# First-half gate weights in units of 256 columns in a GLA + multiplicative-FFN kernel

## Chip, cores, metric

The kernel runs on one core of a Trainium2 chip. The metric is device time in microseconds. Three runs of the kernel before gave 472.68, 473.71 and 473.98 us; the median is 473.71 us. One further execution was profiled: 475.23 us in all, with a span of 473.5 us from its first to its last instruction.

The engines are called PE (TensorE; its weight loads are listed apart as PEld), DVE (VectorE), ACT (ScalarE), POOL (GpSimd) and SP (SyncE, which here only issues transfers). [...]

## The reference

Two blocks follow each other. The first is a gated linear attention, step by step over a sequence of 768, for 4 batches of 8 heads of 48 channels:

```python
for t in range(S):
    state = alpha[:, :, t, :, None] * state + np.einsum('bhd,bhe->bhde', k[:, :, t], v[:, :, t])
    y[:, :, t] = np.einsum('bhd,bhde->bhe', q[:, :, t], state)
```

Its output, as 3072 tokens of 384 channels (x), goes through a feed-forward block without an activation:

```python
a = x @ w1              # 384 -> 1024
b = x @ w2              # 384 -> 1024
h = a * b @ w3          # 1024 -> 1024
return (h @ w_out).astype(np.float32)
```

q, k, v and alpha are float32. The weights w1, w2, w3 and w_out are float64.

## The kernel before, in words

**Part 1: 25 steps over 24 chunks.** The sequence of each batch is cut into chunks of 128 positions: 6 per batch, 24 in all, n = 0 to 23. The main loop (`for n in range(N + 1)`, L634) handles in step n several chunks at once: the scores of chunk n (`scores`, PE L399, masked on DVE at L402 into a tile `ms`), the transposed q and k of chunk n + 1 (`transposed`, PE L359, copied by ACT at L361), the output of chunk n - 1 (`attend_state`, L419, and `attend`, L425, copied by ACT at L429 into a tile `x`), the state update of chunk n (`outer`, PE L371, DVE L379 or L381), the product of q and k with the decays for chunk n + 2 (`decayed`, DVE L337, which is the first reader of the loaded k and q), and the decays of chunk n + 3 (`decays`, PE L318, L321 or L324, and the exponentials on ACT, L327 and L328). The logarithms of alpha (`logs`, ACT L302 or L294) are taken one step ahead of the decays. For every second chunk POOL carries a scaled state over (`advance`, L388 to L390), with factors that go through DRAM and back (L330, L332, L309, then L345).

**Loads.** SP issues nearly all transfers in one order: at the top of step n the stores of an earlier output (`store`, L283), alpha of chunk n + 5 (`load_a`, L142), k and q of chunk n + 3 (`load_kq`, L148 and L149), and weights. v of chunk n + 2 is loaded by POOL for chunks 3 to 7 (L154), otherwise by SP. Three buffers hold k and q, three the alpha of single chunks (chunks 2 to 7 come in pairs and have their own place), five v (`AHEAD` + 1), two the output tile `x`. Each transfer of SP also waits, by a rotation of eight semaphores, for the landing of the one issued eight before it. A row of q, k, v or alpha is 48 floats, 192 B, in DRAM.

**Weights.** w1 and w2 arrive as float64 and are turned into float32 from their two 32-bit words, and then into three parts: h, a rounded top; l, the remainder; m, a second remainder. One unit is a tile of 128 rows and 512 columns (512 KB; a row is 4096 B): rows `kk` of one matrix, one half of the columns. Its generator (`load_gates`, with `to_fp32`) has five stages: issue the load (L213); take the words apart (DVE L222, L225; ACT L221, L226); combine them (DVE L228, L229, L231); h on ACT (L238); l on DVE (L240), which for the second half of the columns also makes m on DVE (L243). For the first half m is made by PE instead (`third`: two matmuls, L254 and L255, and an ACT copy, L256). `fetch` starts loads so that at most `raws` units are begun; `convert(k)` runs k stages. There are 12 units; the first six are the columns 0 to 511, the others columns 512 to 1023.

**Gates.** The tokens form 8 groups g of 384 (three chunks). Once a group's x is complete in DRAM it is loaded (`load_x`, L441) and split in three by `split_x` into the tile `x3`: ACT L447, DVE L448, DVE L449. A gate tile f is 128 of the 1024 columns for one group: for w1 and for w2 nine matmuls (`products`, L455), ACT L464 and DVE L466 take the result out of PSUM, DVE L503 multiplies the two and the product is stored. In part 1 the gate tiles f = 0 to 3 (first half) of the groups 0 to 3 are threaded into the steps in pieces of nine matmuls by `run`. Group 0 starts in step 7 (`FIRST` is 6): two pieces after the transposes, then three more; three in step 8. All eight pieces need units of the first half, and every one of them needs x3 in all three parts.

**Part 2** holds the other gate tiles, the folding of w3 with w_out, and the output products. The change doesn't touch it.

**Order.** The program order is that of the loop, with `after_marks` adding some orders by hand; the Tile framework then fixes the queue of every engine when the program is built. So which instruction stands before which on an engine is known without a run.

Of the kernel before, what the change touches and what calls it, by code (L numbers as in the profile page):

```python
# [48 lines left out]
def kernel(  # L49
# [26 lines left out]
    CW = 512  # L76
    AHEAD = 4
    LATE = 10
# [54 lines left out]
    def load_a(n):  # L133
        if paired(n):
            if n % 2 == 0:
                b, c = divmod(n, NCH)
                x = pairs[n // 2 % 2]
                nc.sync.dma_start(out=x.rearrange("p h s d -> p h (s d)"), in_=alpha[b, :, ds(c * C, 2 * C), :].rearrange("h (p s) d -> p h (s d)", s=2))
                st["a", n] = st["a", n + 1] = x
        elif n < N:  # L140
            st["a", n] = inp.tile([C, H, D], FP32, tag="ac", name="ac")
            nc.sync.dma_start(out=st["a", n], in_=rows(alpha, n))  # L142
# [92 lines left out]
    def load_gates(i, kk, half):  # L235
        w = yield from to_fp32(None, (moe_w1, moe_w2)[i][ds(kk * C, C), ds(half * CW, CW)])
        h, l, m = (w12[half][:, x, i, kk, :] for x in range(3))
        nc.scalar.activation(h, w, AF.Copy, scale=(1.0 - 2.0 ** -13) / P)  # L238
        yield
        mark["l"] = nc.vector.scalar_tensor_tensor(l, h.bitcast(FP32), -P, w, op0=ALU.mult, op1=ALU.add).ins  # L240
        done.append((i, kk, half))
        if half:
            nc.vector.scalar_tensor_tensor(m, h.bitcast(FP32), P + 1.0, w, op0=ALU.mult, op1=ALU.subtract)  # L243
        else:
            thirds.append((m, h, l))

    weights, begun, thirds, done = deque(), deque(), deque(), []

    def third(count):

        for _ in range(count):
            m, h, l = thirds.popleft()
            p = bank()
            nc.tensor.matmul(p, signs[:, 0], h, start=True, stop=False)  # L254
# [109 lines left out]
    def outer(n):  # L364
# [9 lines left out]
        if n % 2:  # L374
            to = st["T", n] = work.tile([C, NP, D], FP32, tag="tmp", name="tmp")
        else:
            to = Ts[1][:, :, 0:D]
# [44 lines left out]
    def attend(n):  # L422
        (y, heads), ms, vc = st.pop(("y", n)), st.pop(("ms", n)), st.pop(("v", n))
        for j, i, to in heads:
            nc.tensor.matmul(to, vc[:, 2 * j + i, :], ms[:, i, j, :], start=(n % NCH == 0 and j % HP == 0),  # L425
                             stop=(j % HP == HP - 1), skip_group_check=True)
        x = work.tile([C, HP, 2, C], FP32, tag="x", name="x")
        for i in range(2):
# [180 lines left out]
    FH = CW // C  # L609
    for half in range(DF // CW):  # L610
        for kk in range(KM):
# [22 lines left out]
    for n in range(N + 1):  # L634
# [3 lines left out]
        if n != 1:  # L638
            load_a(n + 5)
        raws = (3, 3, 3, 3, 2, 2, 3, 3)[n] if n < 8 else 4  # L640
        for m in (n + 3,) * (n <= FIRST) + (n + 4,) * (n >= FIRST):
            load_kq(m)
            if n < FIRST - 2:
                fetch(raws)
            if n >= FIRST:
                load_v(m - 1)
        if n:
# [19 lines left out]
        if n == FIRST:  # L667
            with after_marks("l", ("qkT", n + 1)):
                split_x(0, 0)
            fill.extend(gate(0, f) for f in begin[n - 3][1])  # L670
        pieces = ((3, 3, 2, 0) if n > FIRST + 3 else (0, 3, 3, 0))[(n - FIRST) % 4] if n >= FIRST else 0
        if n == 0:
# [6 lines left out]
        marks = (*[("qkT", n + 1)] * (n < N - 1), *[("qk", n + 1), ("ms", n)] * early, *["x3"] * (n - 2 in begin and n > FIRST))  # L679
        if n < N - 2 and n != FIRST:  # L680
            with after_marks(*marks):
                convert(2 if n == 0 else 1, raws)
        advance(n)
# [3 lines left out]
        third(ready)  # L687
        run(pieces > 0)
        if early:
            with after_marks(*marks):  # L690
                convert(1, raws)
# [5 lines left out]
        if n == 4:  # L697
            load_x(0)
        convert(early and n > 0, raws)
        run(pieces > 1)  # L700
# [5 lines left out]
        if n == FIRST:  # L706
            with after_marks("x3", ("e", n + 3)):
                convert(2, raws)
        elif n < N - 2:
            convert(early or n % 3 == 0, raws)  # L710
        if n == FIRST - 1:
            assert len(done) == 2 * KM
        run(pieces > 2)
# [96 lines left out]
```

## Time and profile before

| | |
|---|---|
| three runs, median | 473.71 us (472.68 to 473.98) |
| profiled execution | 475.23 us, span 473.5 us |
| PE busy / weight loads busy | 457.5 us (97%) / 432.1 us (91%) |
| DVE / ACT / POOL busy | 358.3 / 278.7 / 78.7 us |
| first matmul of a gate (L455) | 59.93 us |
| DVE L449, first x3 complete | 60.42 us, 1.35 us long |
| moved by DMA | 80.29 MB, mean 170 GB/s |
| transfers of w1, w2 and w3 | 28 of 512 KB, median 5.4 us from issue to landing |
| loads of k, of q | 24 each of 192 KB, median 5.1 and 5.6 us |

Busy time of an engine is the time its instructions take; a wait counts as idle, and the profile names what ended it. Matmuls are pipelined, so that their busy time can overlap: 1152 instances of L455 with 338 ns each stand in the trace about every 0.18 us. The chain of waits follows the work that ended last backwards from the end of the program.

### The profile page before, as it was taken

What the parts mean: (1) busy time and instruction counts of PE and PEld (TensorE: products, weight loads), DVE (VectorE), ACT (ScalarE), POOL (GpSimd) and SP (SyncE); (2) the same over time, 40 slices, a digit from 0 to 9 for tenths busy, and PEclk for the clock granted to TensorE, in tenths of its full rate; (3) what the DMA queues carried; (4) which work ended last, traced back from release to release, by engine and by line L of the source; (5) the groups of instructions that cost most, each with busy time, mean ns of one, the idle gap of its engine ahead of it and who ended that gap; (6) DMA issues with size and microseconds to landing.
All of it is one profiled execution on the core that took longest, in us unless ns stands there. A gap on an engine that the chain in (4) does not pass through costs nothing.

```text
span 473.5 us, 10040 instructions
## 1 busy us (share of the span) xinstructions
PE 457.5 (97%) x3848; PEld 432.1 (91%) x3848; DVE 358.3 (76%) x578; ACT 278.7 (59%) x552; POOL 78.7 (17%) x150
## 2 busy tenths in 40 slices
PE   4997899999999999999999999999999999999996
PEld 2675589899989998999999999999999999999996
DVE  2887797999869787999989968854642877666761
ACT  4676864867768464898877765654453533333330
POOL 5243121113201310222221202111011000000000
PEclk9999999999999999999999999999999999999999
DMA  9999999999999933567675532212013986555511
GB/s 181 245 206 227 227 229 201 250 205 208 202 223 184 280 100 122 152 187 242 205 257 178 189 124 89 96 49 85 33 51 98 256 242 184 166 164 169 173 51 50
DMA packets 145663, 80.29 MB, mean 170 GB/s; under 512 B 96240, under 2 KB 137456, under 8 KB 145616
## 3 DMA queue, kind: packets, MB, share of 16 engines
q1 hardware_dynamic: 139840, 64.44, 54.9%
q0 software_dynamic: 5776, 15.22, 10.2%
q8 instruction: 30, 0.49, 0.5%
q14 instruction: 17, 0.14, 0.1%
HBM read 57.58 MB, written 22.06 MB: 168 GB/s over the span
## 4 chain that ended last, share of the span: by engine, by line
PE 87%; DMA 5%; DVE 2%; issue 2%; SPq 2%; ACT 1%; POOL 1%; POOLq 0%; DVEq 0%; ACTq 0%
PE bank L455 71%; PE bank L425 4%; PE bank L399 4%; PE bank L419 2%; PE bank L359 2%; DMA kq<-in_q_dram 2%; PE bank L557 1%; PE bank L371 1%; PE bank L324 1%; DMA dec<-ends 1%; DMA ends<-e 1%; DMA xd<-x 1%; PE bank L321 1%; SPq L149 1%; DMA ac<-in_alpha_dram 1%
## 5 line engine op out<-in xcount | busy, mean ns | idle before, releaser
L455 PE MATMUL bank<-x,w 128*128 128x384 f32 x1152 | 212.1, 338 | 0.6 <-DVE x L449 0.6
L455 PEld LDWEIGHTS bank<-x,w 128*128 128x128 f32 x1152 | 200.1, 188 | 2.9 <-issue 1.4
L455 PE MATMUL bank<-w3o,ab 128*128 128x384 f32 x576 | 100.2, 336 | 0.0
L455 PEld LDWEIGHTS bank<-w3o,ab 128*128 128x128 f32 x576 | 99.9, 188 | 0.0
L480 ACT ACTIVATE bank<-bank 128x384 f32<-128x384 f32 x96 | 45.8, 477 | 41.3 <-PE bank L455 41.1
L464 ACT ACTIVATE t<-bank 128x384 f32<-128x384 f32 x64 | 31.4, 493 | 56.4 <-PE bank L455 55.4
L530 POOL DMA_DIRECT2D abd<-ab x45 | 26.1, 579 | 144.9 <-DVE ab L516 126.1
L516 DVE TENSOR_TENSOR ab<-bank,r 128x384 f32<-128x384 f32 x44 | 24.4, 554 | 25.4 <-ACT bank L480 15.4
L361 ACT COPY qkT<-bank 128x512 f32<-128x512 f32 x48 | 26.0, 593 | 23.4 <-PE bank L359 23.4
L586 DVE TENSOR_TENSOR ab<-abl,ab 128x1024 fp32r<-128x1024 f32 x24 | 29.4, 1224 | 13.1 <-ACT ab L585 13.1
L585 ACT ACTIVATE ab<-abl 128x1024 fp32r<-128x1024 f32 x24 | 25.5, 1061 | 21.2 <-PE bank L455 18.3
L455 PE MATMUL bank<-wo,w3T 128*128 128x384 f32 x192 | 35.9, 334 | 0.0
L455 PEld LDWEIGHTS bank<-wo,w3T 128*128 128x128 f32 x192 | 33.5, 188 | 0.0
L226 ACT ACTIVATE power<-power,rebias 128x512 uint32<-128x512 uint32 (+1 forms) x36 | 25.1, 699 | 12.4 <-DVE power L225 12.2
L337 DVE TENSOR_TENSOR qk<-kq,e 128x768 f32<-128x768 f32 x24 | 22.9, 953 | 12.4 <-ACT e L328 8.4
L399 PEld LDWEIGHTS bank<-qkT 48*128 48x128 f32 x384 | 24.4, 193 | 8.1 <-issue 2.7
L399 PE MATMUL bank<-qkT 48*128 48x128 f32 x384 | 29.3, 291 | 2.4 <-DVE tmp L381 1.8
L402 DVE TENSOR_TENSOR ms<-bank,keep 128x512 int32<-128x512 int32 x48 | 31.2, 683 | 0.4 <-PE bank L399 0.3
L466 DVE SCALAR_TENSOR_TENSOR o<-bank,t 128x384 f32<-128x384 f32 x24 | 13.4, 557 | 22.1 <-issue 13.7
L587 DVE SCALAR_TENSOR_TENSOR ab<-ab,abl 128x1024 fp32r<-128x1024 f32 x24 | 29.2, 1218 | 0.0
L466 DVE SCALAR_TENSOR_TENSOR r<-bank,t 128x384 f32<-128x384 f32 x40 | 22.0, 553 | 8.8 <-PE bank L455 4.1
L425 PE MATMUL bank<-ms,v 128*64 128x128 f32 x384 | 26.3, 279 | 0.0
(88 smaller groups left out, 582.8 us busy)
## 6 DMA issues: line engine op xcount, KB each, us to landing
raw<-in_moe_w_dram SPq DMA_DIRECT2D x28, 512.0 KB, 5.4
abl<-abd SPq DMA_DIRECT2D x24, 512.0 KB, 4.2
abd<-ab POOLq DMA_DIRECT2D x45, 192.0 KB, 3.0
xT<-xd POOLq DMA_DIRECT2D x9, 576.0 KB, 4.6
kq<-in_k_dram SPq DMA_DIRECT2D x24, 192.0 KB, 5.1
kq<-in_q_dram SPq DMA_DIRECT2D x24, 192.0 KB, 5.6
xd<-x SPq DMA_DIRECT2D x48, 96.0 KB, 4.0
out_dram<-o SPq DMA_DIRECT2D x24, 192.0 KB, 3.3
```

The lines of the kernel that those rows point to most:

```text
L361: mark["qkT", n] = nc.scalar.copy(qkT[:, :, :, ds(DP * half, DP)], tp[half]).ins
L399: nc.tensor.matmul(sc[i][:, j, :], qkT[r, 0, j, :], qkT[r, 1, j, :], start=True, stop=True)
L402: masked = nc.vector.tensor_tensor(ms[:, i].bitcast(I32), sc[i].bitcast(I32), keep_bc, op=ALU.bitwise_and)
L425: nc.tensor.matmul(to, vc[:, 2 * j + i, :], ms[:, i, j, :], start=(n % NCH == 0 and j % HP == 0), stop=(j % HP == HP - 1), skip_group_chec ...
L455: nc.tensor.matmul(p, w[part][i], x[part][i], start=start and part == parts[0] and i == 0, stop=stop and part == parts[-1] and i == n - 1, ...
L464: nc.scalar.activation(t, p1, AF.Copy, scale=(1.0 + 1.0 / P) * scale)
L466: nc.vector.scalar_tensor_tensor(to, p2, scale, t, op0=ALU.mult, op1=ALU.add)
L480: nc.scalar.activation(p, p, AF.Copy, scale=1.0 + 1.0 / P)
L530: (nc.gpsimd if late else nc.sync).dma_start(out=abd[g][:, f, :], in_=ab)
L585: nc.scalar.activation(t[:, 0], ab, AF.Copy, scale=1.0 - 2.0 ** -13)
L586: nc.vector.tensor_sub(t[:, 1], ab, t[:, 0].bitcast(FP32))
L587: nc.vector.scalar_tensor_tensor(t[:, 2], t[:, 0].bitcast(FP32), -1.0 - 1.0 / P, ab, op0=ALU.mult, op1=ALU.add)
```

## The change

The first half of the columns is no longer loaded in six units of 128 rows and 512 columns, but in three units of the columns 0 to 255 and three of the columns 256 to 511 (`load_first`). A unit holds two tiles of 128 rows and 256 columns: rows 0 to 255 of w1; rows 0 to 255 of w2; rows 256 to 383 of both. It takes two transfers of 256 KB with rows of 2048 B, where a unit took one of 512 KB with rows of 4096 B. A unit still has 512 numbers per partition, so the stages of its conversion have the same sizes as before. The first three units suffice for the gate tiles 0 and 1, all six for 2 and 3. The units of the second half are as they were.

The schedule is moved with it. Four `convert` calls in each of the steps 0 to 5 become 2, 2, 3, 3, 2 and 4; the step 6 has 3 instead of 2, step 7 has 5 instead of 1. So 16 stages (four units) are through by step 5 instead of 24 (six units), and the other two units are converted in steps 6 and 7; their `third` is in step 8. Step 7 runs four pieces of gates instead of five, step 8 four instead of three. In the last steps of part 1 (`while begun`) five stages of the second half are left instead of two.

The buffers change too: four for v (`AHEAD` 3), and v of chunk n + 2 instead of n + 3 is loaded in the steps from 6 on; two for the single alpha tiles, one for the tile `tmp` of the state update, four for the output tile `x`.

```diff
@@ -74,7 +74,7 @@
     NG = N // G
     TG = G * C
     CW = 512
-    AHEAD = 4
+    AHEAD = 3
     LATE = 10
     PAIRED = 8
     assert D <= DP and DM % C == 0 and DF % CW == 0 and S % C == 0 and N % G == 0
@@ -138,7 +138,7 @@
                 nc.sync.dma_start(out=x.rearrange("p h s d -> p h (s d)"), in_=alpha[b, :, ds(c * C, 2 * C), :].rearrange("h (p s) d -> p h (s d)", s=2))
                 st["a", n] = st["a", n + 1] = x
         elif n < N:
-            st["a", n] = inp.tile([C, H, D], FP32, tag="ac", name="ac")
+            st["a", n] = inp.tile([C, H, D], FP32, tag="ac", name="ac", bufs=2)
             nc.sync.dma_start(out=st["a", n], in_=rows(alpha, n))
 
     def load_kq(n):
@@ -237,20 +237,28 @@
         h, l, m = (w12[half][:, x, i, kk, :] for x in range(3))
         nc.scalar.activation(h, w, AF.Copy, scale=(1.0 - 2.0 ** -13) / P)
         yield
+        nc.vector.scalar_tensor_tensor(l, h.bitcast(FP32), -P, w, op0=ALU.mult, op1=ALU.add)
+        nc.vector.scalar_tensor_tensor(m, h.bitcast(FP32), P + 1.0, w, op0=ALU.mult, op1=ALU.subtract)
+
+    def load_first(c0, k):
+        part = ds(c0, CW // 2)
+        srcs = [((moe_w1, moe_w2)[i], kk) for i in range(2) for kk in range(KM)][k::KM] if k == KM - 1 else \
+            [((moe_w1, moe_w2)[k], kk) for kk in range(KM - 1)]
+        w = yield from to_fp32(None, *(m[ds(kk * C, C), part] for m, kk in srcs))
+        w = w.rearrange("p (a b) -> p a b", a=2)
+        h, l, m = (w12[0][:, x, :, KM - 1, part] if k == KM - 1 else w12[0][:, x, k, 0:KM - 1, part] for x in range(3))
+        nc.scalar.activation(h, w, AF.Copy, scale=(1.0 - 2.0 ** -13) / P)
+        yield
         mark["l"] = nc.vector.scalar_tensor_tensor(l, h.bitcast(FP32), -P, w, op0=ALU.mult, op1=ALU.add).ins
-        done.append((i, kk, half))
-        if half:
-            nc.vector.scalar_tensor_tensor(m, h.bitcast(FP32), P + 1.0, w, op0=ALU.mult, op1=ALU.subtract)
-        else:
-            thirds.append((m, h, l))
-
-    weights, begun, thirds, done = deque(), deque(), deque(), []
+        thirds.append((m, h, l))
+
+    weights, begun, thirds = deque(), deque(), deque()
 
     def third(count):
 
         for _ in range(count):
             m, h, l = thirds.popleft()
-            p = bank()
+            p = bank().rearrange("p (a b) -> p a b", a=2)
             nc.tensor.matmul(p, signs[:, 0], h, start=True, stop=False)
             nc.tensor.matmul(p, signs[:, 1], l, start=False, stop=True)
             nc.scalar.copy(m, p)
@@ -372,7 +380,7 @@
                                  start=True, stop=True)
 
         if n % 2:
-            to = st["T", n] = work.tile([C, NP, D], FP32, tag="tmp", name="tmp")
+            to = st["T", n] = work.tile([C, NP, D], FP32, tag="tmp", name="tmp", bufs=1)
         else:
             to = Ts[1][:, :, 0:D]
         if n % NCH == 0:
@@ -424,7 +432,7 @@
         for j, i, to in heads:
             nc.tensor.matmul(to, vc[:, 2 * j + i, :], ms[:, i, j, :], start=(n % NCH == 0 and j % HP == 0),
                              stop=(j % HP == HP - 1), skip_group_check=True)
-        x = work.tile([C, HP, 2, C], FP32, tag="x", name="x")
+        x = work.tile([C, HP, 2, C], FP32, tag="x", name="x", bufs=4)
         for i in range(2):
             copied = nc.scalar.copy(x[:, :, i], y[i])
         ends_of_part1[1] = copied.ins
@@ -607,7 +615,9 @@
                 fill.popleft()
 
     FH = CW // C
-    for half in range(DF // CW):
+    assert KM == 3 and CW % 4 == 0
+    weights.extend(load_first(c0, k) for c0 in (0, CW // 2) for k in range(KM))
+    for half in range(1, DF // CW):
         for kk in range(KM):
             weights.extend(load_gates(i, kk, half) for i in range(2))
 
@@ -637,13 +647,13 @@
             load_x(loads[n])
         if n != 1:
             load_a(n + 5)
-        raws = (3, 3, 3, 3, 2, 2, 3, 3)[n] if n < 8 else 4
+        raws = (2, 3, 2, 3, 3, 3, 3, 3)[n] if n < 8 else 4
         for m in (n + 3,) * (n <= FIRST) + (n + 4,) * (n >= FIRST):
             load_kq(m)
-            if n < FIRST - 2:
+            if n < FIRST + 2:
                 fetch(raws)
-            if n >= FIRST:
-                load_v(m - 1)
+        if n >= FIRST:
+            load_v(n + 2)
         if n:
             attend_state(n - 1)
         if n < N:
@@ -668,7 +678,7 @@
             with after_marks("l", ("qkT", n + 1)):
                 split_x(0, 0)
             fill.extend(gate(0, f) for f in begin[n - 3][1])
-        pieces = ((3, 3, 2, 0) if n > FIRST + 3 else (0, 3, 3, 0))[(n - FIRST) % 4] if n >= FIRST else 0
+        pieces = ((3, 3, 2, 0) if n > FIRST + 3 else (0, 2, 3, 0))[(n - FIRST) % 4] if n >= FIRST else 0
         if n == 0:
             with after_marks(("qkT", 0)):
                 logs(2)
@@ -677,16 +687,16 @@
                 logs(3)
         early, ready = n < FIRST, len(thirds) if n > 2 else n // 2
         marks = (*[("qkT", n + 1)] * (n < N - 1), *[("qk", n + 1), ("ms", n)] * early, *["x3"] * (n - 2 in begin and n > FIRST))
-        if n < N - 2 and n != FIRST:
+        if n < N - 2:
             with after_marks(*marks):
-                convert(2 if n == 0 else 1, raws)
+                convert((2, 1, 1, 1, 1, 1, 0, 2)[n] if n < 8 else 1, raws)
         advance(n)
         if n:
             attend(n - 1)
         outer(n)
         third(ready)
-        run(pieces > 0)
-        if early:
+        run((pieces > 0) + (n == FIRST + 2))
+        if early and n:
             with after_marks(*marks):
                 convert(1, raws)
         with after_marks(*[("ms", n)] * (n < 3)):
@@ -696,7 +706,7 @@
                 logs(n + 4)
         if n == 4:
             load_x(0)
-        convert(early and n > 0, raws)
+        convert(n in (2, 3, 5), raws)
         run(pieces > 1)
         if n:
             decays(n + 3)
@@ -705,11 +715,9 @@
                 logs(n + 4)
         if n == FIRST:
             with after_marks("x3", ("e", n + 3)):
-                convert(2, raws)
+                convert(3, raws)
         elif n < N - 2:
-            convert(early or n % 3 == 0, raws)
-        if n == FIRST - 1:
-            assert len(done) == 2 * KM
+            convert((0, 0, 0, 0, 0, 1, 3, 3)[n] if n < 8 else n % 3 == 0, raws)
         run(pieces > 2)
         if n == N - 3:
             while begun:
```

## The prediction

> **What bounds the kernel now.** I read the page's table of busy times and its slices first.
>
> ```profile
> PE 457.5 (97%) x3848; PEld 432.1 (91%) x3848; DVE 358.3 (76%) x578; ACT 278.7 (59%) x552; POOL 78.7 (17%) x150
> ...
> PE   4997899999999999999999999999999999999996
> PEld 2675589899989998999999999999999999999996
> ...
> DMA  9999999999999933567675532212013986555511
> ```
>
> PE is the bound, but not from the start: the weight loads stand at 2 to 6 tenths in the first five slices (to 59 us) and at 8 to 9 afterwards. The DMA engines are full for fourteen slices. So I asked for stages: windows of PE, PEld, DVE, ACT and POOL (busy us, instructions), clock, DMA share and GB/s.
>
> ```profile
> 45.00:62.00 17.00, 13.83 (x179) 10.19 (x176) 14.13 (x22) 13.68 (x31) 3.84 (x6) 1.00 0.97 208
> 62.00:75.00 13.00, 13.00 (x155) 12.15 (x156) 12.54 (x24) 7.91 (x19) 3.20 (x7) 1.00 1.09 231
> 90.00:105.00 15.00, 15.00 (x184) 13.85 (x185) 14.77 (x29) 9.10 (x23) 1.49 (x3) 1.00 1.04 233
> ```
>
> From 62 us PE has no idle time worth naming. The change can therefore act in two ways only: by when this dense stretch begins, and by what it adds to PE, or makes it wait for, after that. The chain of waits shows what begins it (start, length, what).
>
> ```profile
> 58.88 0.35 DVE T L379
> 59.24 1.26 DVE x L448
> 60.50 1.28 DVE x L449
> 61.78 0.14 issue
> 61.92 2.33 PE bank L455 x12
> 64.24 1.02 PE bank L425 x16
> ```
>
> PE waits for the last part of x3. I call the end of L449 t0; here it is 61.7. The timeline of DVE says what stands before and after it.
>
> ```profile
> 55.84 0.68 DVE L402 TENSOR_TENSOR ms<-bank,keep 128x512 int32<-128x512 int32 x1
> 58.01 0.96 DVE L337 TENSOR_TENSOR qk<-kq,e 128x768 f32<-128x768 f32 x1 [1.49 <-DMA kq<-in_q_dram]
> 58.88 0.35 DVE L379 COPY T<-bank 128x192 f32<-128x192 f32 x1
> 59.15 1.35 DVE L448 TENSOR_TENSOR x<-xT,x 128x1152 fp32r<-128x1152 f32 x1
> 60.42 1.35 DVE L449 SCALAR_TENSOR_TENSOR x<-x,xT 128x1152 fp32r<-128x1152 f32 x1
> 61.69 0.55 DVE L307 TENSOR_TENSOR la<-la,la 128x384 fp32r<-128x384 f32 x1
> ```
>
> DVE reaches L337 of chunk 8 at about 56.5 and waits 1.49 us for its q; then x3 follows at once. So t0 is set by DVE and, 1.5 us later, by loading. From 61.7 on DVE runs without a gap until 71.7.
>
> **What the Trainium skill says.** "DMA: Bandwidth & Descriptors", Specifications, asks for at least 512 B per transfer for the full rate. The trace agrees: between 62 and 65 us, with mostly 192-B rows, 155 to 185 GB/s; at 68 to 71 us, with weights in rows of 4096 B, up to 437. Halving them to 2048 B leaves them long. The same page, Issuing engines are not separate DMA queues: all queues run on the same 16 engines; a DMA share of 0.97 to 1.09 in the stages above fits. "Perfetto Trace Analysis", Identifying the Most-Contended Engine, advises weight loads and not matmul time for TensorE; here only the former shows the two regimes clearly.
>
> **The change part by part.** Prices on DVE are distances of consecutive starts: L222 0.34, L225 0.33, L228, L229, L240 and L402 0.60 each, L231 0.62, L337 0.87, L379 and L381 0.27, L466 and L503 0.48, L307 0.47.
>
> 1. *Less before t0.* Four units, not six, are converted on DVE before L448. One costs 0.67 + 1.82 + 0.60 = 3.1 us, two 6.2. Not all is won, since other waits come next. I follow the changed queues.
>  - L337 of chunk 5 waited for its load until 37.73. One unit less stands before that load; 0.52 MB at about 380 GB/s is 1.4 us: 36.3. In the changed order it stands before the two L402 of chunk 3, which is harmless: their use is in step 4.
>  - DVE then has L337, two L402, L240, L222 and L225, L381, L228 to L231, L337, two L402, L381, L240: 0.87 + 1.20 + 0.60 + 0.67 + 0.27 + 1.82 + 0.87 + 1.20 + 0.27 + 0.60 = 8.4, to 44.7. POOL's scaled state, needed by the second L381, ended at 43.8; a v load (0.93) leaves its chain and another enters: no help beyond that, and none needed.
>  - Chunk 7's load waits for the landing of chunk 6's (eight transfers back, now that units count double), about 39 to 40, then for a weight piece, about 41.5; with the 5.05 us that it took at most before (44.11 to 49.16), it lands at 46.5, or 48.
>  - From there L337, two L402, the fourth unit with ACT between (3.9) and two L402: 0.87 + 1.2 + 3.9 + 1.2 = 7.2, to 53.7.
>  - Chunk 8's load stands behind alpha of chunk 10, which with two buffers waits for the logarithm of chunk 8. That follows decays of chunk 7 on PE (after L402 at 43.3, 1.5 us), L327 and L328 (0.9) and L302 (0.4): 46.2. With 1 us to the issue of q and 5 to 8.4 us to landing (8.4 from 49.53 before), 52.2 to 55.6. Queued behind that alpha are k and q of 8 and a unit; DVE alone waits for them.
>  - So L337 of chunk 8 starts at about 54.4 instead of 58.01: **a gain of 3.6 us** in t0. Ends: 1.4 (only one unit's transfer) and 5.8 (load at 52.2).
>
> 2. *More after t0.* Units 5 and 6 now stand behind L449. Up to the L240 of unit 6 DVE must do L307, unit 5 (3.1), two L402, two L466, L503, L222 and L225, L381, two L466, L337, L228, L307, L503, L229, an L222 of unit 7, L231, two L402, L240: 0.47 + 3.1 + 1.2 + 0.96 + 0.48 + 0.67 + 0.27 + 0.96 + 0.87 + 0.60 + 0.47 + 0.48 + 0.60 + 0.33 + 0.62 + 1.2 + 0.6 = 13.9 us. PE gets to the two `third` of step 8 sooner: before, step 8's first L455 stood at 74.62, 12.92 after t0, and the nine L455 that leave step 7 took 1.57: t0 + 11.35. The first `third` costs 0.6 (two starts to the next, 0.56 to 0.65). The second one's L255 needs that L240: t0 + 13.95, and ends at 14.2. Before, what then follows would have stood at 11.35. **Loss 2.85**: 1.2 of PE work that lay in idle time before, 1.65 of waiting. Behind L255 queue all of step 8's gates, then step 9.
>  The ACT copy L256 comes after L225 of unit 7 and L226, at about t0 + 16.2; PE wants it ten matmuls after 14.2, at 15.95: **0.3** more. Sum 3.15.
>
> 3. *Transfers.* SP issues six more (0.45 us each at least); SP waited only some 7 us in the first 62, so they cost up to 2.7 if issue binds, 0 if landing does. I take 0: chunk 7 and 8 above are bound by landings. By k and q of chunk 13 both versions have issued ten units; until then the new one is never ahead, so loads in the dense stretch come no later.
>
> 4. *Buffers.* v of chunk n + 2 is now loaded in step n. Before, v of chunk 15 was issued at 109.67 in step 12's place; v of chunk 14 there, 4.5 us to landing, 114.2, is wanted by `outer` at 115.9. Cost 0, with 1.7 us of cover; without it, that wait stops PE directly. `tmp` with one buffer: POOL's read already precedes the next write. `x` with four: removes one ACT wait of 1.6 us that PE doesn't feel.
>
> 5. *Later conversion.* From step 9 DVE's work per step, counted in the changed queue, stays under PE's 8 to 9 us in gate steps (at most 8.6), and steps without gates differ by 1.2 or less. Cost 0, end +1.5.
>
> Sum: -3.6 + 2.85 + 0.3 = **-0.45 us**. The profiled span of 473.5 would be 473.1, its execution 474.8; that execution lay 1.5 us above the median, so against the median, 473.71 becomes **473.3 us**.
>
> **The rivals.** 0.3%, or 1.4 us, is about what a measurement of this kernel can tell from no change.
>
> *Loading still sets t0* (slower). The DMA engines are full before and after; if chunk 8 comes only by the one unit that no longer stands ahead of it, t0 gains 1.4, and the loss of 3.15 in step 8 stays: +1.75, 475.5 us. It decides once t0 gains less than 1.75. For it: the waits for k and q (L337), share 0.97. Against it: DVE, too, was busy 14.1 of 17 us there. The same side has v late in step 14 or a fuller DVE: about +2 on the main case, 475.4.
>
> *Loads come early and DVE alone sets t0* (faster). Fewer outstanding weights shorten the 5 to 8 us from issue to landing; chunk 7 is there at 44.7, chunk 8 at 52.2: gain 5.8, net -2.65, 471.1 us. For it: the first alpha took only 2.99 us in an empty queue. Against it: the rotation of eight and alpha's new wait.
>
> *The new order does nothing* can't quite be: PE's two `third` and DVE's units are moved in the built queues.
>
> **How the numbers follow.** Main case, within 0.3%: 0.42. Slower rivals together 0.33; faster 0.25. I predict the main case, 473.3, whose own range from gains of 2.5 to 4.6 is 472.2 to 474.4. Since both signs share most of the chance, the range takes in both rivals' points and the unknown of step 5: 470.8 to 477.0.
>
> **What would show it.** Right: L449 of group 0 ends at about 58 us, DVE before it with one wait for q; PE idle about 1.7 us at L255 in step 8, released by DVE L240, with L254 and L255 after the transposes of chunk 9; no wait for v. Wrong: L449 later than 60 (the loading step), no wait at L255 (DVE's sum), or idle PE between 75 and 165 us (steps 4 and 5).

## The result, and the profile after

The changed kernel takes 478.85 us (477.83 to 479.29, six runs) where the kernel before took 473.85 beside it: a ratio of 1.0099, interval 1.008 to 1.0117. Repeated with other runs of both, it was 477.57 against 473.40 (1.009, interval 1.0074 to 1.0105). So it is 4 to 5 us slower; the prediction was 473.3, with a range up to 477.0.

The page of the changed kernel, busy times and slices (each digit is the busy share of one fortieth of the span, in tenths):

```profile
PE 457.7 (96%) x3848; PEld 433.5 (91%) x3848; DVE 357.7 (75%) x578; ACT 278.7 (59%) x552; POOL 80.5 (17%) x149
...
PE   4997898999999999999999999999999999999996
PEld 2675697999999999999999999999999999999996
...
PEclk9999899999999999999999999999999999999999
```

Nothing in the sums has moved: PE's busy time differs by 0.2 us, and PE, DVE and ACT run as many instructions as before. What has moved is when the dense stretch begins, and how dense its first part is. One digit is new: PEclk is 8 in the fifth slice (the second profile of the kernel before, below, has such a digit too, in its fourth). The same windows as before (PE, PEld, DVE, ACT, POOL, then clock, DMA share, GB/s):

```profile
45.00:62.00 17.00, 15.21 (x192) 12.55 (x185) 11.66 (x19) 11.90 (x27) 3.83 (x6) 0.90 0.96 208
62.00:75.00 13.00, 11.69 (x145) 10.09 (x144) 13.00 (x26) 9.04 (x21) 3.32 (x7) 1.00 1.05 208
90.00:105.00 15.00, 15.00 (x150) 13.91 (x150) 14.77 (x27) 9.97 (x23) 2.02 (x4) 1.00 1.06 212
```

Before x3, DVE now does less (11.66 us where it did 14.13). From 62 to 75 us the roles are exchanged: PE, which had 13.00 of 13.00, has 11.69, and DVE has 13.00 of 13.00. From 90 us on both kernels look alike.

The timeline of DVE in the changed kernel, ahead of t0 (start, length, line, operation; in brackets the idle time before it and what ended it):

```profile
49.22 0.96 DVE L345 TENSOR_TENSOR qk<-kq,e 128x768 f32<-128x768 f32 x1 [4.67 <-DMA kq<-in_q_dram]
...
55.15 0.69 DVE L252 SCALAR_TENSOR_TENSOR w<-w,mant 128x512 fp32r<-128x512 f32 x1 [0.89 <-ACT w L250]
...
56.95 0.95 DVE L345 TENSOR_TENSOR qk<-kq,e 128x768 f32<-128x768 f32 x1
...
59.35 1.35 DVE L457 SCALAR_TENSOR_TENSOR x<-x,xT 128x1152 fp32r<-128x1152 f32 x1
60.62 0.56 DVE L315 TENSOR_TENSOR la<-la,la 128x384 fp32r<-128x384 f32 x1
```

Lines are 8 higher than in the kernel before for most operations (L337 is L345, L449 is L457). At this point DVE has done three units where the kernel before has done five (up to x3 it is four and six), and it has waited 4.67 us for q of chunk 7. An earlier wait of 4.55 us, for chunk 5, ended at 35.48. t0 is 60.6 us.

The chain of waits shows what made chunk 7 late (start, length, what):

```profile
35.79 5.92 DMA raw<-in_moe_w_dram
...
41.72 7.38 DMA kq<-in_q_dram
...
49.12 0.05 DVEq L345
```

Units 4 and 5 are issued one behind the other, four transfers from 35.79 on. The issue of q of chunk 7 waits for the landing of the first of them, eight transfers back, and q then needs 7.38 us.

What follows t0 stands in PE's timeline of step 8:

```profile
73.42 0.47 PE L262 MATMUL bank<-w,signs 128*128 128x512 f32 x1 [0.67 <-ACT w L250]
74.52 0.50 PE L263 MATMUL bank<-w,signs 128*128 128x512 f32 x1 [0.64 <-DVE w L252]
...
77.03 1.14 PE L463 MATMUL bank<-x,w 128*128 128x384 f32 x5 [0.25 <-ACT w L264]
```

The first `third` of the step starts at 72.01 without a wait; the second waits for h and for l of unit 6, and the gates after it for the copy of m. From 60 us on these are PE's only waits but one of 0.2 us.

I read every run in the same three parts: t0; from t0 to the scores of step 10 (PE L399, now L407); and from there to the end of the span. In the shown profile of the kernel before they are 61.7, 22.9 and 388.9 us, in the changed kernel 60.6, 26.3 and 389.2. That makes +2.6 us, and the medians differ by 5.0. Where are the other 2.4?

### The profile page after: what moved, and what is told of

Read it like the earlier page. It is cut to its first block, busy times and chain, and to the rows that moved or that the text cites. A ratio compares the mean times of both kernels' runs of the same rounds, so it can differ in the third digit from the quotient of the medians.

```text
span 476.1 us, 10055 instructions
## 1 busy us (share of the span) xinstructions
PE 457.7 (96%) x3848; PEld 433.5 (91%) x3848; DVE 357.7 (75%) x578; ACT 278.7 (59%) x552; POOL 80.5 (17%) x149
## 4 chain that ended last, share of the span: by engine, by line
PE 83%; DVE 6%; DMA 4%; ACT 2%; issue 2%; SPq 2%; POOL 1%; DVEq 0%; POOLq 0%; ACTq 0%
PE bank L463 68%; PE bank L407 4%; PE bank L433 3%; DMA kq<-in_q_dram 3%; PE bank L367 2%; PE bank L427 2%; PE bank L565 1%; DMA raw<-in_moe_w_dram 1%; DVE qk L345 1%; PE bank L379 1%; PE bank L332 1%; PE bank L326 1%; PE bank L329 1%; DVE ms L410 1%; SPq L149 1%
## 5 line engine op out<-in xcount | busy, mean ns | idle before, releaser
L463 PE MATMUL bank<-x,w 128*128 128x384 f32 x1152 | 211.5, 338 | 0.4 <-ACT w L264 0.3
L463 PEld LDWEIGHTS bank<-x,w 128*128 128x128 f32 x1152 | 200.3, 188 | 2.2 <-DVE ms L410 0.7
L463 PE MATMUL bank<-w3o,ab 128*128 128x384 f32 x576 | 100.2, 336 | 0.0
L463 PEld LDWEIGHTS bank<-w3o,ab 128*128 128x128 f32 x576 | 99.9, 188 | 0.0
L488 ACT ACTIVATE bank<-bank 128x384 f32<-128x384 f32 x96 | 45.9, 478 | 41.3 <-PE bank L463 41.1
L538 POOL DMA_DIRECT2D abd<-ab x45 | 26.7, 593 | 144.1 <-DVE ab L524 125.7
L345 DVE TENSOR_TENSOR qk<-kq,e 128x768 f32<-128x768 f32 x24 | 23.2, 966 | 20.0 <-DMA kq<-in_q_dram 11.4
L463 PE MATMUL bank<-wo,w3T 128*128 128x384 f32 x192 | 35.9, 334 | 0.0
L226 ACT ACTIVATE power<-power,rebias 128x512 uint32<-128x512 uint32 (+1 forms) x36 | 25.1, 698 | 15.5 <-DVE power L225 15.2
L463 PEld LDWEIGHTS bank<-wo,w3T 128*128 128x128 f32 x192 | 33.5, 188 | 0.0
L410 DVE TENSOR_TENSOR ms<-bank,keep 128x512 int32<-128x512 int32 x48 | 31.0, 683 | 0.9 <-PE bank L407 0.7
L407 PEld LDWEIGHTS bank<-qkT 48*128 48x128 f32 x384 | 24.1, 193 | 5.5 <-issue 2.1
L407 PE MATMUL bank<-qkT 48*128 48x128 f32 x384 | 28.8, 291 | 0.0
```

The source lines that it names most:

```text
L345: mark["qk", n] = nc.vector.tensor_mul(qks[n % 3][:, :, :, 0:D], st.pop(("kq", n)), st.pop(("e", n)).rearrange("p i (h d) -> p i h d", h=H ...
L407: nc.tensor.matmul(sc[i][:, j, :], qkT[r, 0, j, :], qkT[r, 1, j, :], start=True, stop=True)
L410: masked = nc.vector.tensor_tensor(ms[:, i].bitcast(I32), sc[i].bitcast(I32), keep_bc, op=ALU.bitwise_and)
L463: nc.tensor.matmul(p, w[part][i], x[part][i], start=start and part == parts[0] and i == 0, stop=stop and part == parts[-1] and i == n - 1, ...
L488: nc.scalar.activation(p, p, AF.Copy, scale=1.0 + 1.0 / P)
L538: (nc.gpsimd if late else nc.sync).dma_start(out=abd[g][:, f, :], in_=ab)
```

## The experiments

Each run has its own executions of the kernel before beside it, and its loss is counted from these. Beside its own, the changed kernel is 5.0 us slower in one group and 4.2 in the other.

An edit can also move the queues, which are fixed anew when the program is built. In six variants (the buffers alone, unit 5 behind chunk 8 with and without fewer transfers, the light kernel before, alpha behind k and q, more matmuls) the traces have one or two of the products L337 (L345) ahead of t0 at another place in DVE's queue than in the kernel they were made from. Where a reading depends on it, it is said.

### The kernel before, profiled once more

> The kernel before once more, unchanged, to see how its executions spread beside those of the changed kernel (spans 476.1 to 477.5 us, granted clock 0.989 to 0.996 in all six). If the 5.0 us between the medians are of the work itself, its spans lie near 472 us. If a lower granted clock is part of the 5.0 us, all its runs show a clock of 1.000; if the clock has nothing to do with the change, some show 0.99 as well. Median 473.8 us either way.

Measured: 473.38 us, ratio 1.0006 (interval 0.9992 to 1.002). Its DVE ahead of t0:

```profile
30.41 0.96 DVE L337 TENSOR_TENSOR qk<-kq,e 128x768 f32<-128x768 f32 x1 [1.40 <-DMA kq<-in_q_dram]
...
37.67 0.96 DVE L337 TENSOR_TENSOR qk<-kq,e 128x768 f32<-128x768 f32 x1 [0.85 <-DMA kq<-in_q_dram]
...
48.49 0.95 DVE L337 TENSOR_TENSOR qk<-kq,e 128x768 f32<-128x768 f32 x1
...
55.76 0.95 DVE L337 TENSOR_TENSOR qk<-kq,e 128x768 f32<-128x768 f32 x1
...
58.16 1.35 DVE L449 SCALAR_TENSOR_TENSOR x<-x,xT 128x1152 fp32r<-128x1152 f32 x1
59.43 0.55 DVE L307 TENSOR_TENSOR la<-la,la 128x384 fp32r<-128x384 f32 x1
```

No wait at chunk 8, and t0 is 59.4 us, not 61.7. From t0 to step 10 it takes 22.9 us and from there 388.9, both as in the first profile. So the whole difference between the two executions of the same kernel (spans of 473.5 and 471.2) lies ahead of t0. The first is the unusual one: of 27 executions of the kernel before that ran beside this group, the median span was 471.3, and two were longer than 473.5.

Against this second profile the account closes: t0 is 1.2 us later, the stretch to step 10 is 3.4 longer, the rest 0.3: 4.9 us between the spans, where the medians differ by 5.0 and 4.2. The 3.4 is the firmer part, since two profiles of each kernel repeat it within half a microsecond; the 1.2 is a difference of single executions, and t0 of the kernel before moved by 2.3 us between two of them.

The granted clock has little part in these 4.9 us: its mean is 0.996 in both profiles. Over all executions it is 0.995 to 1.000 beside this group and 0.989 to 0.996 in the ten of the changed kernel, so more time at a lower clock comes with the change. Of these ten, the three at 0.989 to 0.991 took 478.63 to 479.29 us, the seven at 0.992 to 0.996 took 477.31 to 479.09. In the kernel before, 13 executions at 0.995 or 0.996 and 17 at a higher clock, beside the lighter loads below, have the same median, 473.38 us.

### The changed kernel, profiled once more

> The changed kernel once more, unchanged: a second profile. Theory (its x3 follows loads, with one long wait each at L345 of the chunks 5 and 7): t0, the end of L457 of group 0, between 59.5 and 62 us, those two waits together 7 to 10 us, from t0 to the scores of step 10 26 to 27.5 us, time 478.5. If the first profile was an odd one, t0 comes under 59 us or the waits under 4 us.

Measured: 477.57 us. t0 is 60.15 us, the two waits at L345 are 4.98 and 4.15 us, t0 to step 10 takes 26.7, the rest 389.2. The first profile of the changed kernel was no odd one.

### The buffers alone, in the kernel before

```diff
-    AHEAD = 4
+    AHEAD = 3
-            st["a", n] = inp.tile([C, H, D], FP32, tag="ac", name="ac")
+            st["a", n] = inp.tile([C, H, D], FP32, tag="ac", name="ac", bufs=2)
...
-            if n >= FIRST:
-                load_v(m - 1)
+        if n >= FIRST:
+            load_v(n + 2)
```

(and one buffer for `tmp`, four for `x`).

> The kernel before with the changed buffers alone: four for v with the load of chunk n + 2 in step n, two for single alpha tiles, one for tmp, four for x. Theory (buffers cost nothing): 473.8 us within 0.7, no wait for v. Rival (part of the unexplained 2.4 us of the median comes from the buffers, and from v above all): 1 to 2.5 us more, with PE waiting at L371 or L425 for v, or at L399 later in the steps 12 to 16.

Measured: 472.64 us beside 473.04, ratio 0.9991 (interval 0.9973 to 1.0008); no wait of PE for v. In the kernel before the buffers cost nothing; in the changed kernel they were not tested by themselves.

### Unit 5 behind chunk 8

```diff
-        raws = (2, 3, 2, 3, 3, 3, 3, 3)[n] if n < 8 else 4
+        raws = (2, 3, 2, 2, 2, 3, 3, 3)[n] if n < 8 else 4
```

> The changed kernel, but the two transfers of unit 5 are issued behind k and q of chunk 8 instead of ahead of those of chunk 7; the queues of PE, ACT and POOL are the same. Theory (the second unit in front delays chunk 7, and chunk 7 sets the start of the gates): DVE L345 of chunk 7 starts at about 46.8 us instead of 49.2, L457 of group 0 ends at about 58.2 instead of 60.6, and the time falls by 2.4 us, to about 476.4. Rival (chunk 7 comes late because the DMA engines are full anyway): 49 and 60.6 us as before, 478.9. Second rival (the gain is eaten where unit 5 is converted, because its transfer is now late there): 58.2 us, but the two matmuls L263 of step 8 no earlier than at 74.5 us, 478.9.

Measured: 478.32 us, ratio 1.0105 (interval 1.0081 to 1.013): no gain. DVE's timeline:

```profile
48.12 0.96 DVE L345 TENSOR_TENSOR qk<-kq,e 128x768 f32<-128x768 f32 x1 [3.17 <-DMA kq<-in_q_dram]
...
54.65 0.96 DVE L345 TENSOR_TENSOR qk<-kq,e 128x768 f32<-128x768 f32 x1 [1.48 <-DMA kq<-in_q_dram]
```

Chunk 7 comes 1.1 us earlier, not 2.4 (1.7 earlier counted from chunk 5, which came 0.6 later in this execution), and then chunk 8 is waited for: t0 is 60.1. The unit that stands in front is a smaller part of chunk 7's delay than I thought. The wait for chunk 8 is in part made by the build: L345 of chunk 8 stands here ahead of L252 and two L410, in the changed kernel behind them. These take 1.8 us, so that in the old order the 1.48 us could have been filled (an estimate from the two timelines). The run shows that the unit delays chunk 7; it doesn't show that moving it is worth nothing.

### Five units before x3

```diff
-                convert(1, raws)
-        with after_marks(*[("ms", n)] * (n < 3)):
+                convert(3 if n == FIRST - 1 else 1, raws)
+        with after_marks(*[("ms", n)] * (n < 3), *["l"] * (n == FIRST - 1)):
             decayed(n + 2)
...
-            convert((0, 0, 0, 0, 0, 1, 3, 3)[n] if n < 8 else n % 3 == 0, raws)
+            convert((0, 0, 0, 0, 0, 3, 3, 1)[n] if n < 8 else n % 3 == 0, raws)
```

(and two stages less at the top of step 7, so that the sum stays; `raws` is 2 in the steps 5 and 6).

> The changed kernel, but five units instead of four are converted before x3: unit 4 stands ahead of L345 of chunk 7, where DVE is idle for 4.7 us, and unit 5 takes the place that unit 4 had. Theory (the loss after x3 is the conversion of two units behind it): L457 of group 0 still ends at about 60.6 us, no wait at L262 or L263 in step 8, one pair of them less there; 1.3 + 0.3 of waiting and 0.6 of PE work go: 2.2 us less, about 476.6. Rival (the fifth unit pushes the start of the gates back, as six did before): L457 ends 1.5 to 3 us later, 478 to 480.

Measured: 480.67 us (477.43 to 482.85), ratio 1.0162 (interval 1.0132 to 1.0192): slower. In its profile, which is of its shortest execution, t0 is 59.1 with one unit more done, so the rival fell in this profile: DVE had the room. The wait at L262 and L263 is gone, too. But in step 9 PE waits 2.42 us for a mask, and DVE's timeline says why:

```profile
79.68 0.56 DVE L511 TENSOR_TENSOR ab<-r 128x384 f32<-128x384 f32 x1
83.92 0.43 DVE L222 TENSOR_SCALAR mant<-raw 128x512 uint32<-128x512 uint32 x1 [3.68 <-DMA raw<-in_moe_w_dram]
84.26 1.28 DVE L410 TENSOR_TENSOR ms<-bank,keep 128x512 int32<-128x512 int32 x2
```

DVE reaches a later unit before its load has landed, and the mask L410 stands behind that L222 in the fixed queue: PE had finished the scores for it at 80.1, and it starts at 84.26. My expectation had priced the stall that goes and not the load that is late next. What makes the other executions 1.5 to 5.4 us longer than this one no profile shows; their clock is 0.985 to 0.995, that of the profile 1.000.

### Lighter loads, in both kernels

In both kernels of v of the chunks 3 to 7 one head of eight is loaded (and POOL clears the v buffers from the fourth on as a whole at the start):

```diff
-            (nc.gpsimd if 2 < n < 8 else nc.sync).dma_start(out=st["v", n][:, :, 0:D], in_=rows(v, n))
+            (nc.gpsimd if 2 < n < 8 else nc.sync).dma_start(out=st["v", n][:, 0:1 if 2 < n < 8 else H, 0:D], in_=rows(v, n)[:, 0:1 if 2 < n < 8 else H])
```

> The kernel before, but of v of the chunks 3 to 7 only one head of eight is loaded (24 KB instead of 192 KB each, 0.84 MB less before 50 us; the other heads are zeros or old values). Theory (in the kernel before, DVE's work sets the end of the first x3, called t0, and loads add 2 us at most): t0 falls from 59.4 or 61.7 us to about 57 and the time to about 471 us. Rival (loads set t0 there too): t0 falls by 4 us or more, to 55.5, the time to 469.

> The changed kernel with the same five loads of v cut to one head. Theory (with four units instead of six DVE is done early and waits for loads, so t0 follows them): the waits of 4.6 and 4.7 us at L345 of the chunks 5 and 7 shrink to under 2 us each, t0 falls from 60.6 us to 54 or 55, and the time by about 6 us, to 473: no slower than 2 us above the light kernel before, where the difference is 5.0 us with whole loads. Rival (something else than loads sets t0 in the changed kernel): t0 falls by less than 2 us, the time stays over 476.8.

Measured: the kernel before stays where it was, 473.44 beside 473.38 us (ratio 1.0, interval 0.9989 to 1.0012), with t0 at 60.3. It did not fall to 471, as I had expected. The changed kernel takes 475.85 us, ratio 1.004 (interval 1.0022 to 1.0059): 2.5 us above the kernel before instead of 4.2 to 5.0. So about 2 us come back, a third of what I expected. Its DVE:

```profile
45.62 0.96 DVE L345 TENSOR_TENSOR qk<-kq,e 128x768 f32<-128x768 f32 x1 [2.75 <-DMA kq<-in_q_dram]
...
53.36 0.95 DVE L345 TENSOR_TENSOR qk<-kq,e 128x768 f32<-128x768 f32 x1
...
57.03 0.55 DVE L315 TENSOR_TENSOR la<-la,la 128x384 fp32r<-128x384 f32 x1
```

The waits at chunks 5 and 7 shrink from 4.55 and 4.67 to 3.04 and 2.75 us, and t0 moves by 3.6, to 57.0. The stretch to step 10 stays at 26.4 us. So loads set t0 in the changed kernel.

That they have no part in the kernel before doesn't follow from its light version, because its queue is another one:

```profile
42.38 0.96 DVE L337 TENSOR_TENSOR qk<-kq,e 128x768 f32<-128x768 f32 x1 [2.42 <-DMA kq<-in_q_dram]
43.26 1.28 DVE L402 TENSOR_TENSOR ms<-bank,keep 128x512 int32<-128x512 int32 x2
```

This is L337 of chunk 6. In the kernel before it stands behind these two masks, L222 and L225; here it stands ahead of them, so that DVE waits 2.42 us with 1.9 us of work behind it, and PE waits 3.39 us for the mask. What lighter loads alone would do in the kernel before stays open. What its second profile shows is how far off the loads are: the last wait for one ends at 37.67, and from there DVE is its own limit for 21.8 us up to t0 (but for 2.0 us of waiting for ACT). In the changed kernel the last such wait ends at 49.22, and 11.4 us remain. The bound moves from DVE's work to the loads, by degrees.

### Units 5 and 6 not converted, and both causes away

```diff
+        if c0 and k:
+            next(to_fp32(None, *(m[ds(kk * C, C), part] for m, kk in srcs)))
+            for x in range(4):
+                yield
+            return
         w = yield from to_fp32(None, *(m[ds(kk * C, C), part] for m, kk in srcs))
```

> The changed kernel without the conversion of the units 5 and 6: they are still loaded, but their h, l and m are zeros, written at the start, so DVE has 6.2 us less to do after x3 and step 8 has no L262, L263 and L264. Theory (all that is lost after x3 comes from these two units): t0 stays near 60.6 us, from there to the scores of step 10 it takes 22.9 us as in the kernel before, instead of 26.3; the time falls by 3.4 us, to 475.4. Rival (the later loads, or the gates' new place, cost too): more than 24 us from t0 to step 10, over 476.5.

Measured: 477.24 us (475.73 to 480.26), ratio 1.0085 (interval 1.0047 to 1.0123): 3.9 us above the kernel before. By the time alone a gain over the changed kernel is not clear. In its profile (of an execution of 475.99 us) t0 is 60.55 and the stretch to step 10 takes 24.1 us: 2.2 of the 3.4 are gone, 1.1 are not. The scores tell where. From those of step 8 to those of step 10 the changed kernel takes 17.97 us and this run 14.67; the kernel before takes 13.12 and runs one piece of nine matmuls less there, 1.57. So in these two steps, where the conversion was expected to cost, it costs 3.3 us, and without it nothing is left. The 1.1 lie ahead of step 8: PE had none of the gate's matmuls done at t0, because it stood still for 3.18 us before (for the mask behind chunk 7) and then ran at half its clock until about 58 us.

> The changed kernel with both suspected causes taken away: of v of the chunks 3 to 7 one head of eight is loaded, and the units 5 and 6 are loaded but not converted (their h, l and m are zeros). Theory (late loads and the conversion behind x3 make up all of the 5.0 us, and they add): t0 at 57.0 as with light loads alone, 22.9 us from there to the scores of step 10, time 475.85 - 3.4 = 472.4, that is 1.0 below the kernel before. Rival (there is a third cause): 474 or more.

Measured: 474.47 us (471.97 to 477.07), ratio 1.0021 (interval 0.9997 to 1.0045). So with both away the changed kernel is nearly at the kernel before, but 2.1 us above what I expected; the rival, at 474 or more, was the better guess. The interval includes no difference at all, so a third cause isn't shown either. Its profile is of its longest execution, 477.07 us. There t0 is 57.6, the scores of step 10 start at 81.1, 1.2 us ahead of the second profile of the kernel before, and then this is lost: DVE waits 3.60 and 4.32 us at L226 (L222 in the changed kernel) for loads of later units, PE 2.55 us for DVE, and PE's clock is at half from 84 to 90 us. This tells what that execution lost, not the median. It is the late load of the run with five units again, which an emptier DVE meets; in the changed kernel itself DVE waited for such a load once between 58 and 84 us, for 1.2.

### Six more transfers in the kernel before, and four fewer in the changed one

```diff
-        w = yield from to_fp32(None, (moe_w1, moe_w2)[i][ds(kk * C, C), ds(half * CW, CW)])
+        w = yield from to_fp32(None, *((moe_w1, moe_w2)[i][ds(kk * C, C), ds(half * CW + c, CW if half else CW // 2)] for c in ((0,) if half else (0, CW // 2))))
```

> The kernel before, but each of its first six units comes in two transfers of 256 KB with rows of 2048 B instead of one of 512 KB with rows of 4096 B; all else is the same. Theory (the shape of the transfers costs nothing): 473.4 us within 0.7. Rival (six more issues on SP and the rotation of eight delay k and q): t0 1 us or more later, 474.4 to 476.

Measured: 475.60 us beside 473.40, ratio 1.0048 (interval 1.0034 to 1.0061). Two transfers in place of one cost the kernel before 2.2 us. In its profile t0 is 60.7, between those of the two profiles of the kernel before; 1.8 us are lost behind step 10, of which PE waits 1.1 for ACT L429. The changed kernel loses only 0.3 there, so that these 2.2 us can't be carried over to it.

```diff
-        w = yield from to_fp32(None, *(m[ds(kk * C, C), part] for m, kk in srcs))
+        w = yield from to_fp32(None, *((m[ds(kk * C, C), part] for m, kk in srcs) if k == KM - 1 else [srcs[0][0][0:2 * C, part].rearrange("(a p) n -> p a n", a=2)]))
```

> The changed kernel, but the four units whose two tiles come from one matrix are each loaded by one transfer of 512 KB (still in rows of 2048 B) instead of two of 256 KB; SP issues four transfers less, the other queues are the same. Theory (the number of transfers is part of the loss, as in the kernel before, where six more cost 2.2 us): four sixths of that come back, the waits of 4.2 to 5.0 us at L345 of the chunks 5 and 7 shrink by a microsecond or more in sum, t0 falls to about 59 us and the time by 1.5 us, to about 476.5. Rival (bytes and rows set the loads, not the number of transfers): t0 60 to 61, time 477.5 to 478.9.

> The same, and unit 5 is loaded behind chunk 8 instead of ahead of chunk 7, which by itself moved t0 by only 0.5 us and the time by nothing clear (e1_unit5_late). Theory (the two effects add): t0 about 58.5 us; but the 26.3 us from there to the scores of step 10 stay or grow by the 0.9 that e1_unit5_late showed, so the time is 476 to 477, and nothing that is done to the loads brings the changed kernel below the kernel before. Rival (with the loads out of the way the change gains): under 474.

Measured: 477.71 us (ratio 1.0103, interval 1.0088 to 1.0118) with four transfers fewer, which is no change, t0 at 59.9; and 476.84 us (1.0083, interval 1.0069 to 1.0097) with unit 5 moved as well, 3.9 above the kernel before. In the latter t0 is 58.3, the earliest of all variants with whole loads, and the stretch to step 10 grows to 28.5: step 10 starts at 86.8, as in the changed kernel (86.9). PE's timeline says where the gain goes:

```profile
58.84 5.18 PE L463 MATMUL bank<-x,w 128*128 128x384 f32 x18
```

PE had waited 1.63 us for L252 just before. The first gates start 0.5 us after t0, where in the changed kernel they start 0.75 ahead of it, and these 18 matmuls take 5.18 us instead of 3.39: the clock is at half from 56 to 62.8 us. The waits for the conversion in step 8 are no longer than in the changed kernel (0.63 and 0.26 us). So an early t0 was worth nothing here because PE was late and slow for it. How much of the 5.0 us the six additional transfers make stays open: adding them costs the one kernel 2.2, taking four away returns nothing to the other.

### Alpha behind k and q in the kernel before

```diff
-        if n != 1:
+        if n < 2 and n != 1:
             load_a(n + 5)
...
+        if n > 1:
+            load_a(n + 5)
```

> The kernel before, but from step 2 on alpha of chunk n + 5 is issued behind k and q of chunk n + 3, v and the weights of that step. If loads of k and q still cost the kernel before a microsecond before x3, t0 falls by about 1 us, to 58.4, and the time to 472.0. If DVE's work alone sets t0, 473.0 within 0.5.

Measured: 475.37 us, ratio 1.0042 (interval 1.0027 to 1.0057). t0 is 59.4, as without it (with L337 of the chunks 6 and 7 at other places of the queue), and later ACT waits 13.9 us in sum at L302 for alpha. The load that is moved back comes due elsewhere. None of the variants is faster than the kernel before.

### More matmuls where PE is idle

```diff
+        if n == FIRST:
+            p = bank().rearrange("p (a b) -> p a b", a=2)
+            for i in range(5):
+                nc.tensor.matmul(p, signs[:, 0], w12[0][:, 0, 0, 0:KM - 1, 0:CW // 2], start=i == 0, stop=i == 4)
```

> The changed kernel with five more matmuls of 128x512 whose output nothing reads, in front of the state output of step 6, where PE stood idle for 1.63 us before its clock was halved from 53.4 to 56.7 us. Theory (an idle PE brings the lower clock on, and the lower clock makes PE late for the first gates): the clock stays 1.000 in most runs, and the time falls by 0.5 to 1.5 us, to about 477.5. Rival (the clock has another cause, or no weight): the clock spreads from 0.989 to 0.996 as before, the time stays within 0.5 us of the changed kernel or rises by up to 1.6 us.

Measured: 480.56 us (478.01 to 483.03), ratio 1.0149 (interval 1.0104 to 1.0194): slower than the changed kernel, the clock from 0.989 to 0.999. In its profile the clock holds through 52 to 58 us, but it is halved behind the next waits, those of step 8 (PE's windows: busy us, instructions, clock, DMA share, GB/s):

```profile
72.00:74.00 2.00, 0.69 (x2) 1.00 1.03 344
74.00:76.00 2.00, 2.00 (x8) 0.54 1.11 335
76.00:78.00 2.00, 2.00 (x9) 0.60 0.97 130
```

The 27 gate matmuls L463 there take 6.43 us instead of 4.95 (the run without units 5 and 6, at full clock). With the fill the clock stayed up in one place and fell in another, where 1.5 us of gates are lost to it. The profile is of the shortest execution, 478.01 us; why others took up to 483 it doesn't show.

## Why the prediction was wrong, point by point

**The reading of the bound** held: PE is dense from t0 on, and only t0 and what is added behind it count. From step 10 on the two kernels differ by 0.3 us. Two of its readings are a little off and nothing rests on them: the weight loads stand at 2 to 7 tenths in the first five slices, not 2 to 6, and in slices of 0.15 us the rate from 62 to 65 us is 96 to 280 GB/s, not 155 to 185.

**Step 1, less before t0, failed**, in two places: it has a gain of 3.6 us where the profiles show a loss of 1.2. Its bullet on chunk 7 took "the 5.05 us that it took at most before" from issue to landing and had it land at 46.5 or 48. The issue came when it said (41.72 us for 41.5, set by the weight piece, although q of chunk 6 landed at 41.1 and not at 39 to 40), chunk 5 was ready 0.8 earlier than it said (35.48 for 36.3), but q needed 7.38 us and was there at 49.1. Why 7.38 is shown in part: without unit 5 in front chunk 7 came 1.1 us earlier, with light loads of v 3.6 earlier; the rest stays open. From L345 of chunk 7 to that of chunk 8 DVE needed 7.73 us for 7.2, with 0.89 of waiting for ACT. Together t0 is 60.6, not 58.1. The bullet after it, chunk 8's load behind the two alpha buffers, never became the limit: in the changed kernel DVE does not wait for chunk 8. "L449 later than 60 (the loading step)" was named as a sign of being wrong, and it came: x3 ends at 60.6.

The second place is what the gain was measured from. The prediction read 61.7 as the t0 of the kernel before and the 1.49 us at chunk 8 as a wait that a change could remove. It said itself that the execution lay 1.5 us above the median, and took that off the end as a constant. The second profile has t0 at 59.4 and no such wait. Of the 2.3 us between the two t0, 1.5 lay in the very wait that was to be won. From 59.4 the predicted t0 of 58.1 would have been a gain of 1.3, and the sum +1.8 us; with the measured 60.6 it is a loss of 1.2.

**Step 2, more after t0, was right**: a loss of 3.15 predicted, 3.4 measured in one profile (3.8 in the other). DVE's sum of 13.9 us gave L255 (now L263) at t0 + 13.95; it starts at t0 + 13.90 (14.3 in the second profile). The wait for L256 (now L264) was to be 0.3 us and is 0.25. Of the 1.65 us foreseen at L255, 1.31 came, in two pieces, 0.67 at L262 for h of unit 6 and 0.64 at L263 for l. That this is the conversion's doing the run without it shows: from step 8 to step 10 it is 3.3 us shorter.

**Step 3, transfers at nothing**: that splitting is free is refuted for the kernel before, which it costs 2.2 us. For the changed kernel, which the step is about, it stays open: four transfers fewer returned nothing, and "2.7 if issue binds, 0 if landing does" was not decided. **Step 4, buffers at nothing**: right, as far as the kernel before shows it. **Step 5, later conversion at nothing**: right within 0.3 us.

**The rivals.** "Loading still sets t0" is what happened, and the light loads show it for the changed kernel, where about 2 us come back. Its size was off, +1.75 for 5.0, because it still began from 61.7 and gave one unit's transfer as a sure gain. The faster rival, DVE alone, needs chunk 7 at 44.7 us; even with light loads it came at 45.6. The range ended at 477.0 since none of its cases had t0 later than before.

In one sentence: the change takes 6.2 us of work from DVE ahead of x3, DVE spends them waiting for q (9.2 us in the two waits from 28 us on, where the kernel before in its second profile waited 2.3), and the same 6.2 us then stand behind x3, where PE waits for them.

## What to carry to other kernels

Work taken off an engine ahead of a point is a gain only if the next arrival at that point is earlier as well; list every transfer that stands in front of that arrival, with the time from issue to landing in the new order, not the old one. Before a wait in a profile is counted as something to win, look whether a second execution has it: the surplus of one execution over the median sits in some wait, and it may be that one. Work moved behind such a point lands on whichever engine is full there, and its price is the sum of that engine's queue: here 13.95 us foretold, 13.90 and 14.3 measured. And compare the queues of a variant with those of its original before a wait in it is read: the edit may have moved them.

## What the runs showed of the hardware

PE's clock fell to half for 3.4 us at a time in five of the profiles (both of the changed kernel, the second of the kernel before, unit 5 behind chunk 8, more matmuls) and for about 6.8 us in three (units 5 and 6 not converted, both causes away, four fewer transfers with unit 5 late), after idle stretches that were shorter than that. In the changed kernel:

```profile
50.00:52.00 2.00, 1.00 (x16) 1.00 1.13 274
52.00:54.00 2.00, 2.00 (x31) 0.82 0.97 180
54.00:56.00 2.00, 2.00 (x25) 0.50 0.92 174
56.00:58.00 2.00, 2.00 (x24) 0.83 0.92 271
```

PE stood idle for 1.6 us, from 49.2 to 50.8, and its clock was halved from 53.4 to 56.7 us, when it was busy again. The Trainium skill, "TensorE: Matmul & The Clock Gate", Part 1, gives a window of about 3.4 us that runs freely and a half rate after an idle window. The length agrees; but a window that was idle for less than half was enough here, and an equal wait at another place (1.57 us, ending at 43.1) brought nothing. So a wait of PE can cost more than its length, some microseconds later. Where it comes decides what it costs: ahead of t0 in the changed kernel it cost nothing, since from L345 of chunk 7 to t0 DVE needs 11.40 us there and 11.41 in the light version, whose clock stayed at 1.00; under the first gates of the run with four fewer transfers and unit 5 late it made 18 matmuls 1.8 us longer.
